# Column tiles, two-head key tails, eight single PSUM banks and a new order in a Performer and mixer kernel

## Chip, cores and metric

The kernel runs on one core of a Trainium2 chip. The metric is the device time of one execution in microseconds (us), as the median of several. The kernel before takes 291.5 us, the median of three runs (291.33 to 291.67).

## What is computed

Eight batches go through linear attention with random features (eight heads, sequence 576, head size 64, 128 features) and then, as a 576 x 512 matrix per batch, through a mixer: a two-layer MLP over tokens (576 to 256 to 576), added to its input, then one over channels (512 to 1536 to 512), added to its input.

```python
def phi(x):
    proj = np.einsum('bhsd,md->bhsm', x, omega)
    h = proj - np.sum(x * x, axis=-1, keepdims=True) / 2.0
    h = h - np.max(h, axis=-1, keepdims=True)
    return np.exp(h) / np.sqrt(m)
q_p, k_p = phi(q * scale), phi(k * scale)
kv = np.einsum('bhsm,bhsd->bhmd', k_p, v)
z = np.sum(k_p, axis=2)
x = np.einsum('bhsm,bhmd->bhsd', q_p, kv) / (np.einsum('bhsm,bhm->bhs', q_p, z)[..., None] + 1e-06)
...
h = np.maximum(x.transpose(0, 2, 1) @ w_tok1, 0.0) @ w_tok2
u = x + h.transpose(0, 2, 1)
out = u + np.maximum(u @ w_ch1, 0.0) @ w_ch2
```

The maximum in phi cancels for q. For k it is divided out row by row: the kernel takes the maximum of the exponentials, and scales v's row and a column of ones by its reciprocal.

## The kernel before

The 576 tokens are 512 main tokens and 64 tail tokens. Every matmul operand is fp16; accumulation is in fp32 in PSUM[...]. The kernel holds six single banks (`bank`, L227) and one `pair` of two (L228).

All work is written as jobs for a planner (L38 to L174): each has an engine, a cost, a key, jobs it depends on, and buffers it takes and gives back. At build time the planner runs a model of the engines: it always picks the job that can start first, and of equals the one with the lowest key. So the order on each engine comes from the costs, the keys (L17 to L20) and the number of buffers, and it is fixed in the program. Until the first heavy channel matmul, the planner fills gaps on TensorE (PE) longer than 0.3 us with dummy matmuls on zeros (L925). A row-tiled job just after another has its key lowered by `ks` (L119).

Per batch and pair of heads (`attention`, L504):

- `kp` (L617) and `qp` (L631) project two heads' k and q on the features. k and q lie transposed, in two halves of 64 partitions, so each matmul uses 64 rows of the array, and two of them run side by side in row tiles.
- ScalarE (ACT) takes the exponential out of PSUM (L500). VectorE (DVE) takes k's maxima (`km`, L643) and reciprocals; GpSimd (POOL) scales v (`vs`, L650).
- `kv` (L663) sums k'v over the main tokens. L670 adds the tails: the tail rows of four heads stand in 128 rows (two tokens of each head in the halves `e`), so each pair of heads needs two matmuls of 130 columns, against `vbd`, v's tails laid out block by block for four heads by POOL (L577).
- `num` (L698, L700) is the numerator with its denominator as a 65th column; DVE divides (L707, L708). From batch 2 on both heads of a pair go into one `pair` of banks and are divided together; in batches 0 and 1 each head has a bank of its own.

k's tails have their own projection `kt` (L532), from `ktt`, a copy that POOL makes out of the transposed k (L366). The tails of q are `qt` (L592). Both write the `pair`.

Batches 0 and 1 are loaded as they are, and PE transposes them (L471, L491). From batch 2 on (`dma_in`), POOL's queue casts q and k to fp16 into DRAM (L355), and SP's queue reads them back transposed (L363). POOL's DMAs are issued in program order and rotate over eight lanes, so one waits until the DMA eight places before it has landed.

The token MLP (`token_mix`, L730; `token_mix_first` for batch 0, in blocks of 128 columns, L781 to L799) gives `u`; SP transposes u by DMA (L762) into `uT`. The 64 tail tokens of two batches are done together in `token_tail` (L807): `w2t` holds the 64 tail columns of w_tok2 twice, once padded to the left half of 128 columns and once to the right, so batch `2p` lands in rows 0 to 63 of one bank and batch `2p + 1` in rows 64 to 127, by four full matmuls. The channel MLP (`channel_mix`, L823) is L832 (first layer, 12 blocks), L852 (relu on ACT), L870 (second layer) and L879 (sum on DVE); SP stores the result. The main tokens of the eight batches take eight passes of it, the tails of all batches a ninth.

POOL's queue also makes two small copies (`touch`, L373, and `touch_u`, L379) that stand between a finished buffer and the next load.

Of the kernel before, what the change touches and what calls it, by code (L numbers as in the profile page):

```python
# [9 lines left out]
FP32 = mybir.dt.float32  # L10
# [6 lines left out]
KEYS = {"a": -1.353, "as": 0.087, "t": -0.936, "ts": 0.381, "gv": 2.14, "lt": -2.027, "lv": -1.831, "to": -1.942, "tt": 0.315, "ks": 1.1, "km": 0.226, "vs": -0.618, "l1": -0.809, "kt": -0.077}  # L17
NEAR = {"1": {"a": -2.195, "as": 0.095, "t": -1.803, "ts": 0.0, "gv": 0.044, "km": -1.819, "vs": -0.475, "kt": -0.001}, "2": {"a": -1.272, "as": 0.154, "t": -0.769, "ts": 0.144, "gv": 1.686, "km": 3.821, "vs": 1.759, "lv": -1.566, "lt": -1.734, "kt": 0.022}}
HEAD = {"kp": [-3.838, -3.822, -3.798, -3.404], "ke": [-2.728, -2.927, -2.827, -2.727], "km": [-4.039, -3.592, -4.221, -2.75], "vs": [-3.332, -3.487, -3.196, -3.14], "qp": [-3.203, -3.403, -3.303, -3.503], "qe": [-3.328, -3.374, -3.028, -3.748], "kv": [-3.533, -3.228, -3.003, -3.133], "ko": [-3.081, -3.035, -3.463, -3.354], "n": [-3.199, -3.199, -3.182, -3.099, -2.999, -3.268, -2.999, -2.899], "no": [-4.124, -3.426, -3.326, -3.144, -3.226, -3.426, -3.126, -2.386], "ktm": -3.64, "kt": -5.022, "kte": -3.991, "qt": -3.751, "qte": -4.323, "kx": [-6.213, -5.658, -5.558, -5.458], "kxo": [-5.931, -7.05, -5.718, -4.783], "ktx": -6.15, "ktxo": -5.753, "qx": [-5.449, -2.792], "qxo": [-4.073, -3.081], "qtx": -5.093, "qtxo": -3.371, "t1": [-0.475, -0.755, -0.539, -0.445], "re": [-0.129, -0.781, 0.181, 0.341], "ut": [-0.17, -0.48, -0.104, -0.64], "uo": [-0.099, -0.259, -0.108, 0.211], "vbd": -8.97, "w1": -9.8, "w1t": -9.38, "w2t": -8.94, "wa": -9.39, "wb": -9.17, "w2": -8.13}
# [18 lines left out]
class Planner:  # L38
# [37 lines left out]
    def run(self):  # L76
# [6 lines left out]
        while any(waiting.values()):  # L83
            choice = None
            for eng, jobs in waiting.items():
                ready = []
                for j in jobs:
# [31 lines left out]
                    key = j.key - (KEYS["ks"] if eng == "PE" and j.rows and last_rows else 0.0)  # L119
# [58 lines left out]
def kernel(  # L178
# [40 lines left out]
    def ring(n, shape, dt, name):  # L219
# [3 lines left out]
             "kvsb": 3, "ktt": 2, "x": 3, "r1": 3, "u": 3, "uT": 3, "r3": 2, "o": 4, "bank": 6, "pair": 1}  # L223
# [4 lines left out]
    pairs = [pspool.tile([P, 2, 512], FP32, name=f"pair{i}") for i in range(COUNT["pair"])]  # L228
# [7 lines left out]
    mask = sb([P, 4], FP16, "mask")  # L236
    w1m = sb([P, NJ, DT], FP16, "w1m")
    w1t = sb([P, 2, DT], FP16, "w1t")
    w2t = sb([P, NT, 2, P], FP16, "w2t")
# [53 lines left out]
    def pair(name):  # L293
        return pairs[place("pair", name)]

# [44 lines left out]
    def load_v_tail(b, key, deps=()):  # L340
        jobs = []
        for g in range(2):
            def tails(g=g):
                nc.gpsimd.dma_start(
                    out=t_vt[place("vt", b)][:, g, :],
                    in_=v[b, 4 * g : 4 * g + 4, SM:S, :].rearrange("h (r e) d -> h r (e d)", e=2),
                )
            jobs.append(dma("POOL", key + 0.01 * g, 0.22, tails, take=[("vt", b)], deps=deps, cost=0.7))
        ld["vt", b] = jobs[-1]

    def load_transposed(b, key, deps=()):
        casts = []
        for n, w in enumerate("qk"):
            def cast(w=w):
                nc.gpsimd.dma_start(  # L355
                    out=scratch[w, b].rearrange("(p r) e -> p (r e)", p=P),
                    in_=src[w][b].rearrange("h s d -> (h s d)").rearrange("(p f) -> p f", p=P),
                )
            casts.append(dma("POOL", key + 0.01 * n, 3.2, cast, deps, cost=0.55))
        for n, w in enumerate("qk"):  # L360
            def back(w=w):
                t = (t_qT if w == "q" else t_kT)[place(w + "T", b)]
                nc.sync.dma_start_transpose(out=t.unsqueeze(1), in_=scratch[w, b])  # L363
            ld[w + "T", b] = dma("SP", key + 0.2 + 0.01 * n, 2.2, back, deps=casts, take=[(w + "T", b)], cost=2.5)
        def ktt():
            nc.gpsimd.tensor_copy(out=t_ktt[place("ktt", b)].rearrange("p (h r) -> p h r", h=H),  # L366
                                  in_=t_kT[place("kT", b)].rearrange("p (h r) -> p h r", h=H)[:, :, R:RA])
        ld["ktt", b] = add("POOL", 0.4, key + 0.25, ktt, deps=[ld["kT", b]], take=[("ktt", b)], give=[("kT", b)])
# [41 lines left out]
    j_mask = add("DVE", 0.7, -8.0, lambda: [nc.vector.memset(mask, 0.0)] + [nc.vector.memset(mask[32 * i : 32 * i + 32, i : i + 1], 1.0) for i in range(4)])  # L410
    j_w1tz = add("DVE", 0.3, -7.9, clear(w1t))
    j_w2tz = add("DVE", 0.3, -7.8, clear(w2t))
# [45 lines left out]
    def rows_of(b, w):  # L458
        return (t_qT if w == "q" else t_kT)[place(w + "T", b)].rearrange("p (h r) -> p h r", h=H)
# [44 lines left out]
    def attention(b, key, step):  # L504
# [15 lines left out]
        def two(n):  # L520
            return [pair(n)[:, e] for e in range(2)]
        def two_of(n):
            return [("pair", n)]
        if dma_in:
            j_ktt = ld["ktt", b]
        else:
            j_ktt = tr["kt", b]
        def kt():
            ps, t = two(n_kt), t_ktt[place("ktt", b)]
            for g in range(2):  # L530
                for e in range(2):
                    nc.tensor.matmul(ps[e][:, g * M : (g + 1) * M], t[half[e], g * P : (g + 1) * P], omT[half[e]], start=True, stop=True)  # L532
        j_kt = add("PE", mm(2, P), k0, kt, deps=[j_ktt, j_omT], take=[*two_of(n_kt), ("kpt", b)], give=[("ktt", b)], rows=True)
        if b == 0:
# [6 lines left out]
            for e in range(2):  # L541
# [4 lines left out]
                j_kte.append(add("ACT", 0.45, kkt, kt_exp, deps=[j_ktm], take=[("kpt", b)], give=[("pair", n_kt)]))  # L546
# [11 lines left out]
        else:  # L558
            def kt_exp():
                exp(t_kpt[place("kpt", b)].rearrange("p g e m -> p e g m"), pair(n_kt)[:, :, 0 : 2 * M].rearrange("p e (g m) -> p e g m", g=2))  # L560
            j_kte = [add("ACT", 0.5, kkt, kt_exp, deps=[j_kt], take=[("kpt", b)], give=[("pair", n_kt)])]
            def kt_max():
# [3 lines left out]
                with nc.allow_low_precision(reason="fp16 operand of the matmul"):  # L566
                    nc.vector.reciprocal(out=rc, in_=mx)
                nc.vector.tensor_tensor(  # L568
                    out=vb[:, :, :, D],
                    in0=rc.unsqueeze(2).broadcast_to((P, 4, 4)),  # L570
                    in1=mask.unsqueeze(1).broadcast_to((P, 4, 4)),
                    op=ALU.mult,
                )
            j_ktm = add("DVE", 1.2, kkt + 0.01, kt_max, deps=[*j_kte, j_mask], take=[("vbd", b)])
            def vbd():
                vb = t_vbd[place("vbd", b)]
                nc.gpsimd.tensor_tensor(  # L577
                    out=vb[:, :, :, 0:D],
                    in0=t_vt[place("vt", b)].rearrange("p g (e d) -> p (g e) d", e=2).unsqueeze(2).broadcast_to((P, 4, 4, D)),
                    in1=vb[:, :, :, D : D + 1].broadcast_to((P, 4, 4, D)),  # L580
                    op=ALU.mult,
                )
            j_vbd = add("POOL", 1.95, kkt + 0.02, vbd, deps=[j_ktm, ld["vt", b]], give=[("vt", b)])
# [10 lines left out]
        def qt_exp():  # L594
            o = t_qpt[place("qpt", b)][:, ST : ST + SM].rearrange("p (h r e) -> p e h r", h=H, e=2)
            exp(o, pair(n_qt)[:, :, 0:256].rearrange("p e (h r) -> p e h r", h=H))
        j_qte = [add("ACT", 0.5, kqe, qt_exp, deps=[j_qt, j_pads], take=[("qpt", b)], give=[("pair", n_qt)])]

        last_x = []
        for hp in range(NU):  # L600
# [57 lines left out]
            def kv(hp=hp, n_kv=n_kv):  # L658
# [10 lines left out]
                for e in range(2):  # L669
# [4 lines left out]
            j_kv = add("PE", mm(8, 65) + mm(2, 130), at_["kv"], kv, deps=[j_v, *j_tail, *je], take=[("bank", n_kv), ("kvsb", (b, hp))],  # L674
# [10 lines left out]
            alone = b < NPE  # L685
            for hs in ((0,), (1,)) if alone else ((0, 1),):
                n_h = (n_n, hs)
                at = ("bank" if alone else "pair", n_h)
                def where(n_h=n_h, hs=hs):
                    return bank(n_h).unsqueeze(1) if len(hs) == 1 else pair(n_h)  # L690
# [116 lines left out]
    def token_tail(pair_, key, jr, jx):  # L807
        n = ("htt", pair_)
        def go():
            ps = bank(n)  # L810
            for o in range(2):
                for tb in range(NT):
                    nc.tensor.matmul(ps, w2t[:, tb, o, :], t_r1[place("r1", 2 * pair_ + o)][:, tb, :],  # L813
                                     start=(o == 0 and tb == 0), stop=(o == 1 and tb == NT - 1))
        j1 = add("PE", mm(4, 512), key, go, deps=[*jr, j_w2t], take=[("bank", n)], give=[("r1", 2 * pair_), ("r1", 2 * pair_ + 1)])
# [82 lines left out]
    def w2t_copy():  # L898
        for o in range(2):
            nc.gpsimd.tensor_copy(out=w2t[:, :, o, o * ST : (o + 1) * ST], in_=w2[:, :, SM:S])  # L900
    j_w2t = add("POOL", 0.6, HEAD["w2t"], w2t_copy, deps=[j_w2, j_w2tz])
# [7 lines left out]
    for b in range(B):  # L909
        if b >= NPE:  # L910
            load_transposed(b, b + key_of("lt", b), [touched.get(b - 2)])
            load_v_tail(b, b + key_of("lt", b) + 0.02)
            load_v(b, b + key_of("lv", b), [ld["ktt", b]] + ([touch_u(1, b + key_of("lv", b) - 0.1, added[1])] if b == NPE else []))
# [44 lines left out]
```

## Time and profile before

| what | us |
|---|---|
| median of three runs | 291.5 |
| the profiled execution | 291.6 |
| its span, first to last instruction | 289.8 |
| channel MLP, first layer, L832, full tokens: matmuls x duration | 376 x 0.379 |
| channel MLP, second layer, L870, 512 columns | 420 x 0.380 |
| tail part of kv, L670, 130 columns | 64 x 0.219 |
| tails of token mixing, L813, 512 columns | 16 x 0.380 |
| ACT exponential of 128 x 512, L500, mean | 0.61 to 0.62 |
| DVE division of a pair of heads, L707 and L708 | 0.215 and 0.824 |
| DVE division of one head, L707 and L708 | 0.187 and 0.492 |
| POOL `vbd`, L577 | 1.928 |
| POOL `ktt`, L366 | 0.398 |
| POOL issue of v's tails, L344 | 0.708 |

The durations of matmuls overlap, since a matmul starts before the one ahead of it has drained; differences of starts tell what one costs. The profile names lines of the kernel before. The granted clock of PE was full throughout.

### The profile page before, as it was taken

To read this page: it belongs to the slowest core of one execution; us is meant where nothing else is said; L and a number is where in the kernel's file an instruction comes from. 1 tells how busy PE (TensorE), PEld (TensorE's weight loads), DVE (VectorE), ACT (ScalarE), POOL (GpSimd) and SP (SyncE) were. 2 spreads that over 40 slices of the span, in tenths; PEclk is the share of its full clock that TensorE was granted. 3 is DMA by queue.
4 is the path that set the end of the run, shared out by engine and by line. 5 is a ranking of instruction groups with operands and counts; after the bars stand their busy time and mean duration, and the time that the engine had idled before them with its cause. 6 is when DMAs were issued, how large, how long until landed. Compare 5 with 4: busy or idle time off the path is not lost.

```text
span 289.8 us, 5517 instructions
## 1 busy us (share of the span) xinstructions
PE 283.2 (98%) x2207; PEld 143.6 (50%) x2207; DVE 147.9 (51%) x280; ACT 153.3 (53%) x307; POOL 91.0 (31%) x116
## 2 busy tenths in 40 slices
PE   8999999999999999999999999999999999999993
PEld 4576454445544544465445544554455444444442
DVE  3985974476469524854657246645565231111012
ACT  2993981298367554855466646653765402512600
POOL 8995920247017401740274016501430000000000
PEclk9999999999999999999999999999999999999999
DMA  8999999799975997999767976998511043012014
GB/s 193 190 199 189 203 226 171 138 220 175 162 125 143 191 118 144 185 193 193 99 153 156 211 100 110 189 199 128 119 74 38 0 96 123 2 49 112 2 35 109
DMA packets 75737, 39.57 MB, mean 137 GB/s; under 512 B 54976, under 2 KB 70720, under 8 KB 75328
## 3 DMA queue, kind: packets, MB, share of 16 engines
q0 software_dynamic: 24304, 17.43, 41.2%
q1 hardware_dynamic: 50624, 21.01, 33.0%
q10 hardware_dynamic: 784, 0.79, 0.9%
q8 instruction: 17, 0.28, 0.4%
q14 instruction: 8, 0.07, 0.1%
HBM read 35.88 MB, written 16.52 MB: 181 GB/s over the span
## 4 chain that ended last, share of the span: by engine, by line
PE 93%; ACT 3%; DMA 1%; issue 0%; DVE 0%; DVEq 0%
PE bank L870 33%; PE bank L832 31%; PE bank L737 4%; PE bank L754 4%; PE bank L617 3%; PE bank L663 3%; PE bank L631 2%; PE pair L698 2%; PE bank L471 2%; ACT kp L500 1%; PE bank L813 1%; PE bank L670 1%; PE bank L738 1%; ACT qp L500 1%; DMA omega_nat<-in_omega_dram 1%; PE bank L781 1%
## 5 line engine op out<-in xcount | busy, mean ns | idle before, releaser
L870 PE MATMUL bank<-wc,r 128*128 128x512 f16 (+2 forms) x444 | 101.5, 374 | 0.0
L852 ACT ACTIVATE r<-bank 128x512 f16<-128x512 f32 x106 | 63.4, 602 | 70.3 <-PE bank L832 69.7
L832 PE MATMUL bank<-uT,wc 128*128 128x512 f16 x376 | 90.1, 379 | 0.3 <-ACT kp L500 0.2
L870 PEld LDWEIGHTS <-r 128*128 128x128 f16 x444 | 40.4, 98 | 47.5 <-issue 5.1
L832 PEld LDWEIGHTS <-wc 128*128 128x128 f16 x424 | 39.3, 98 | 42.4 <-issue 1.2
L500 ACT ACTIVATE qp<-bank 128x512 f16<-128x512 f32 x64 | 35.7, 624 | 13.9 <-PE bank L631 13.8
L643 DVE TENSOR_REDUCE km<-kp 128x8 f16<-128x1024 f16 x32 | 38.6, 1208 | 7.7 <-ACT kp L500 7.7
L500 ACT ACTIVATE kp<-bank 128x512 f16<-128x512 f32 x64 | 34.3, 611 | 10.5 <-PE bank L617 10.5
L650 POOL TENSOR_TENSOR vs<-v,vs 128x512 f16<-128x512 f16 x32 | 33.5, 1057 | 15.4 <-DVE vs L645 11.9
L879 DVE TENSOR_TENSOR o<-u,bank 128x512 f32<-128x512 f16 x28 | 19.1, 681 | 28.1 <-PE bank L870 28.1
L757 DVE TENSOR_TENSOR u<-x,bank 128x512 f16<-128x512 f16 x28 | 17.4, 683 | 9.1 <-PE bank L754 9.1
L577 POOL TENSOR_TENSOR vbd<-vt,vbd 128x1024 f16<-128x1024 f16 x7 | 13.5, 1928 | 26.9 <-DVE vbd L568 23.3
L366 POOL COPY ktt<-kT 128x256 f16<-128x256 f16 x6 | 2.4, 398 | 58.1 <-DMA kT<-k 58.1
L708 DVE TENSOR_TENSOR x<-pair,rc 128x640 f16<-128x640 f32 x24 | 19.8, 824 | 0.8
L707 DVE RECIPROCAL rc<-pair 128x10 f32<-128x10 f32 x24 | 5.2, 215 | 22.4 <-PE pair L700 22.4
L698 PEld LDWEIGHTS <-qp 128*128 128x128 f16 x256 | 12.9, 98 | 6.1 <-issue 0.4
L745 DVE TENSOR_SCALAR r<-bank 128x512 f16<-128x512 f32 x7 | 4.8, 692 | 19.1 <-PE bank L738 19.1
L737 PE MATMUL bank<-x,w1m 128*128 128x512 f16 x56 | 14.4, 379 | 0.0
L663 PEld LDWEIGHTS <-kp 128*128 128x128 f16 x256 | 11.1, 98 | 5.4 <-ACT qp L500 0.6
L663 PE MATMUL bank<-vs,kp 128*128 128x65 f16 x256 | 13.0, 193 | 0.4 <-ACT qp L500 0.4
L754 PE MATMUL bank<-r,w 128*128 128x512 f16 x56 | 13.2, 379 | 0.0
L617 PE MATMUL bank<-omT,kT 64*128 64x128 f16 x256 | 12.1, 218 | 0.0
(109 smaller groups left out, 276.9 us busy)
## 6 DMA issues: line engine op xcount, KB each, us to landing
out_dram<-o SPq DMA_DIRECT2D x32, 256.0 KB, 2.5
q<-in_q_dram POOLq DMA_DIRECT2D x6, 576.0 KB, 6.8
k<-in_k_dram POOLq DMA_DIRECT2D x6, 576.0 KB, 10.0
wc<-in_moe_w_ch_dram POOLq DMA_DIRECT2D x4, 768.0 KB, 10.9
v<-in_v_dram POOLq DMA_DIRECT2D x6, 512.0 KB, 5.9
r<-in_q_dram POOLq DMA_DIRECT2D x4, 256.0 KB, 7.6
v<-in_v_dram POOLq DMA_DIRECT2D x4, 256.0 KB, 7.5
out_dram<-o SPq DMA_DIRECT2D x5, 128.0 KB, 2.4
```

The costliest lines, as they stand in the source:

```text
L500: nc.scalar.activation(out=out, in_=in_, func=AF.Exp, bias=0.0, scale=1.0)
L617: nc.tensor.matmul(ps[e][:, c : c + M], m[half[e], r, :], omT[half[e]], start=True, stop=True)
L643: nc.vector.reduce_max(out=mx, in_=kpv, axis=AX.X)
L650: nc.gpsimd.tensor_tensor(out=vs[:, :, 0:D], in0=t_v[place("v", b)][:, hh[0] : hh[0] + 2, :].rearrange("p h (j d) -> p (h j) d", d=D), in1 ...
L663: nc.tensor.matmul(ps[:, i, :], kpv[:, 2 * i + j // 2, j % 2, :], vs[:, i * NJ + j, 0 : D + 1], start=(i == 0 and j == 0), stop=False, ski ...
L708: nc.vector.tensor_tensor(out=t_x[place("x", b)][:, :, (2 * hp + hs[0]) * D : (2 * hp + hs[0] + n) * D].rearrange("p j (i d) -> p i j d", ...
L737: nc.tensor.matmul(ps, w1m[:, j, tb * P : (tb + 1) * P], x[:, j, :], start=(j == 0), stop=False)
L754: nc.tensor.matmul(ps, w2_of(tb, j), r1[:, tb, :], start=(tb == 0), stop=(tb == NT - 1))
L832: nc.tensor.matmul(ps, wc1[:, db, cb * P : (cb + 1) * P], moving(db), start=(db == 0), stop=(db == ND - 1))
L852: nc.scalar.activation(out=o, in_=bank(n), func=AF.Relu)
L870: nc.tensor.matmul(ps[:, cols], r3[:, cb, j * P : (j + 1) * P], wc2[:, cb, cols], start=(cb == 0), stop=(cb == NCB - 1))
L879: nc.vector.tensor_tensor(out=t_o[place("o", (c, j))][:, cols], in0=uu[:, cols], in1=bank(n)[:, cols], op=ALU.add)
```

## The change

- `token_tail` uses w2's 64 tail columns as they are, for two column tiles: batch `2p` writes PSUM rows 0 to 63 and batch `2p + 1` rows 64 to 127, alternating. The buffer `w2t`, its clearing and its copies go.
- From batch 2 on, k's tails lie by two heads in 128 rows. The cast of k becomes three DMAs: two for the tails (heads 0 to 3, and 4 to 7, side by side in the scratch tensor), and one for the main tokens. `kt` reads the tail part of the transposed k, so POOL's copy `ktt` is not made. The tail part of kv is one matmul for a pair of heads; `vbd` covers two heads for each pair (`mask2`), and v's tails are loaded to match it. Batches 0 and 1 keep the old layout.
- PSUM is eight single banks. Exponentials of k's and q's tails become two instructions each, one for a bank. All numerators go head by head and are divided head by head.
- The keys of the planner are new throughout, and the key bonus `ks` needs the same kind of tiles as the job before. The order on every engine is new. Dummy matmuls become 26 instead of 20.

```diff
-                    key = j.key - (KEYS["ks"] if eng == "PE" and j.rows and last_rows else 0.0)
+                    key = j.key - (KEYS["ks"] if eng == "PE" and j.rows and last_rows == j.rows else 0.0)
...
-             "kvsb": 3, "ktt": 2, "x": 3, "r1": 3, "u": 3, "uT": 3, "r3": 2, "o": 4, "bank": 6, "pair": 1}
+             "kvsb": 3, "ktt": 2, "x": 3, "r1": 3, "u": 3, "uT": 3, "r3": 2, "o": 4, "bank": 8}
...
-                nc.gpsimd.dma_start(
-                    out=t_vt[place("vt", b)][:, g, :],
-                    in_=v[b, 4 * g : 4 * g + 4, SM:S, :].rearrange("h (r e) d -> h r (e d)", e=2),
-                )
+                if b < NPE:
+                    o, i = t_vt[place("vt", b)][:, g, :], v[b, 4 * g : 4 * g + 4, SM:S, :].rearrange("h (r e) d -> h r (e d)", e=2)
+                else:
+                    o = t_vt[place("vt", b)][g * ST : (g + 1) * ST].rearrange("p a (c d) -> p (a c) d", c=2)
+                    i = v[b, :, SM:S, :].rearrange("(a i) t d -> i t a d", i=2)[g]
+                nc.gpsimd.dma_start(out=o, in_=i)
...
-            casts.append(dma("POOL", key + 0.01 * n, 3.2, cast, deps, cost=0.55))
+            def cast_main(w=w):
+                nc.gpsimd.dma_start(
+                    out=scratch[w, b][0 : H * R].rearrange("(p r) e -> p (r e)", p=P),
+                    in_=src[w][b, :, 0:SM, :].rearrange("h s d -> h (s d)").rearrange("h (c f) -> h c f", c=P // H),
+                )
+            def cast_tail(w=w):
+                for g in range(2):
+                    nc.gpsimd.dma_start(
+                        out=scratch[w, b][H * R : H * RA, g * D : (g + 1) * D],
+                        in_=src[w][b, 4 * g : 4 * g + 4, SM:S, :],
+                    )
+            if w == "k":
+                casts.append(dma("POOL", key + 0.01 * n - 0.005, 0.8, cast_tail, deps, cost=1.1))
+            casts.append(dma("POOL", key + 0.01 * n, 3.2, cast if w == "q" else cast_main, deps, cost=0.55))
...
-        def ktt():
-            nc.gpsimd.tensor_copy(out=t_ktt[place("ktt", b)].rearrange("p (h r) -> p h r", h=H),
-                                  in_=t_kT[place("kT", b)].rearrange("p (h r) -> p h r", h=H)[:, :, R:RA])
...
-            ps, t = two(n_kt), t_ktt[place("ktt", b)]
+            ps, t = two(n_kt), t_kT[place("kT", b)][:, H * R : H * RA] if dma_in else t_ktt[place("ktt", b)]
...
-            j_kte = [add("ACT", 0.5, kkt, kt_exp, deps=[j_kt], take=[("kpt", b)], give=[("pair", n_kt)])]
+            nh = 2 if dma_in else 4
+            msk, j_msk = (mask2, j_mask2) if dma_in else (mask, j_mask)
+            j_kte = []
+            for e in range(2):
+                def kt_exp(e=e):
+                    o = t_kpt[place("kpt", b)]
+                    exp(o[:, e] if dma_in else o[:, :, e], two(n_kt)[e][:, 0 : 2 * M].rearrange("p (g m) -> p g m", g=2))
+                j_kte.append(add("ACT", 0.3, kkt, kt_exp, deps=[j_kt], take=[("kpt", b)], give=[("bank", (n_kt, e))]))
...
-                    in0=t_vt[place("vt", b)].rearrange("p g (e d) -> p (g e) d", e=2).unsqueeze(2).broadcast_to((P, 4, 4, D)),
-                    in1=vb[:, :, :, D : D + 1].broadcast_to((P, 4, 4, D)),
+                    in0=t_vt[place("vt", b)].rearrange("p g (e d) -> p (g e) d", e=2).unsqueeze(2).broadcast_to((P, 4, nh, D)),
+                    in1=vb[:, :, :, D : D + 1].broadcast_to((P, 4, nh, D)),
...
-                for e in range(2):
+                if dma_in:
+                    nc.tensor.matmul(ps, kt_[:, hp // 2, hp % 2, :], vb[:, hp, 0:2, 0 : D + 1], start=False, stop=True, skip_group_check=True)
+                for e in () if dma_in else range(2):
                     nc.tensor.matmul(
...
-            alone = b < NPE
-            for hs in ((0,), (1,)) if alone else ((0, 1),):
+            for hs in ((0,), (1,)):
...
-            for o in range(2):
-                for tb in range(NT):
-                    nc.tensor.matmul(ps, w2t[:, tb, o, :], t_r1[place("r1", 2 * pair_ + o)][:, tb, :],
-                                     start=(o == 0 and tb == 0), stop=(o == 1 and tb == NT - 1))
-        j1 = add("PE", mm(4, 512), key, go, deps=[*jr, j_w2t], take=[("bank", n)], give=[("r1", 2 * pair_), ("r1", 2 * pair_ + 1)])
+            for tb in range(NT):
+                for o in range(2):
+                    nc.tensor.matmul(ps[half[o]], w2[:, tb, SM:S], t_r1[place("r1", 2 * pair_ + o)][:, tb, :],
+                                     start=(tb == 0), stop=(tb == NT - 1))
+        j1 = add("PE", mm(2, 512), key, go, deps=[*jr, j_w2], take=[("bank", n)], give=[("r1", 2 * pair_), ("r1", 2 * pair_ + 1)], rows="cols")
```

In the changed file `kt` is L540, `qt` L605, `kp` L632, `qp` L646, `kv` L678 with its tails L685 (batches 2 to 7) and L687, the numerators L714 and L716, the token tails L829, the channel MLP L848 and L886.

## The prediction

> **What bounds the kernel now.** I read the busy shares first, then the chain that ended last, then busy time by stretch, then TensorE in order of time, and last the queues that feed it. The page:
>
> ```profile
> PE 283.2 (98%) x2207; PEld 143.6 (50%) x2207; DVE 147.9 (51%) x280; ACT 153.3 (53%) x307; POOL 91.0 (31%) x116
> ...
> PE 93%; ACT 3%; DMA 1%; issue 0%; DVE 0%; DVEq 0%
> ```
>
> The chain is TensorE. Ends of matmuls are modelled, so I asked for stretches (start:end, length, busy time of PE, PEld, DVE, ACT, POOL, clock, DMA share, GB/s):
>
> ```profile
> 0.00:24.50 24.50, 22.61 (x251) 15.04 (x252) 16.46 (x48) 16.67 (x42) 22.49 (x36) 1.00 1.17 192
> 24.50:62.00 37.50, 37.18 (x337) 19.27 (x335) 23.77 (x50) 21.02 (x43) 12.78 (x17) 1.00 1.12 185
> 62.00:285.00 223.00, 223.00 (x1618) 109.02 (x1617) 107.00 (x183) 115.57 (x224) 55.70 (x65) 1.00 0.66 123
> ```
>
> From 62 us on PE is never idle, and from 24.5 to 62 it lacks 0.3 us. So there time goes only with PE's own work; in the first 24.5 us it goes with what feeds PE. What a step of PE costs is read from starts (start us, us, engine, line):
>
> ```profile
> 60.22 0.38 PE L870 MATMUL bank<-wc,r 128*128 128x512 f16 x1
> 60.53 0.40 PE L617 MATMUL bank<-omT,kT 64*128 64x128 f16 x8
> 60.86 1.04 PE L813 MATMUL bank<-r,w2t 128*128 128x512 f16 x4
> 61.83 0.39 PE L631 MATMUL bank<-qT,omT 64*128 64x512 f16 x2
> 62.20 1.24 PE L832 MATMUL bank<-uT,wc 128*128 128x512 f16 x5
> ```
>
> The second column is modelled; the first is not. Four L813 start at 60.86 and the next thing at 61.83: 0.97 = 4 x 0.216 + 0.10. From L870 to L617 it is 0.31 = 0.216 + 0.095. So a 128x512 matmul takes 0.216 us, and each change between full and row-tiled matmuls about 0.094. The same differences give 57 ns for a 130-column matmul, 29 ns for one of 65 columns.
>
> **The skill.** The Trainium skill, "TensorE: Matmul & The Clock Gate", section "Measured speedup vs the span model", has tiles side by side last as long as one, plus about 4 ns for each further, columns within 5 ns of rows. The trace agrees for rows (both L631 matmuls start 3 ns apart); it shows no column tiles. "TensorEngine Tiling (Array Packing)", "Key Properties", says a change of mode drains the array: the trace's 0.094 us. Its "Restrictions" say column tiling turns fast weight load off: not shown here, a load is 98 ns under a 216 ns matmul. "DMA: Bandwidth & Descriptors", "Why small descriptors are slow (HBM only)", charges every descriptor a fixed part, 27% at 256 bytes; the trace has no load in rows of 256 bytes; v's tails, 32 KB in rows of 512, take 9.6 us to land, mostly in the queue.
>
> **The change part by part.** PE's work, from the changed instruction order times those durations:
>
> 1. k's tails by two heads: 24 of 64 130-column matmuls go (batches 2 to 7): 24 x 0.057 = -1.37.
> 2. Tails of token mixing: four times 4 x 0.216 = 0.86 becomes two pairs of 0.22, 0.44: -1.70 in all. If columns did not overlap: 0; if they go faster than one stream: excluded. First weight load in the open at worst 4 x 0.1. I take -1.70.
> 3. Changes of mode: row visits fall from 43 to 38, four column visits come, three of them touching row visits; borders 86 to 80: -6 x 0.094 = -0.56. A row/column border was never traced; between 0 and 0.19 each; I take 0.094.
>
> Sum -3.63. All numerators, projections and mixing stay.
>
> Times in the new order, below, are PE's instructions in their new order with these durations laid end to end from the point that I work out next; where a feeder is later than that, I add a wait by hand.
>
> The start. In the old order PE begins batch 1's transposes of k (L471) at 24.54 with all four token-mix blocks of batch 0 done; in the new order two blocks (each 4 x 0.109 + 0.216 + 0.22 = 0.87) come later. Equal progress would be 24.54 - 1.74 = 22.80. ACT and DVE feed PE there. ACT's list up to its second scaling of a head is the same, but one relu (0.27) moves behind that scaling and qp's tail is split in two (+0.1): it ended at 20.02, so now near 19.9. On it waits a product of the first token mix (10 matmuls of 56 ns, 0.56); then stand a second product, a block, a third product whose last head DVE has near 21.2, and a block: 19.95 + 3 x 0.56 + 2 x 0.87 = 23.4. k of batch 1 has to be there too: issued at 13.00, 10.0 us to landing, 23.0. On POOL, vbd (1.9) now goes ahead of w1 and w2, and k's issue slips by 0.2; the DMA engines are full meanwhile (share 1.17), which hides it; without that cover it is 0.2 more, still in time. So 23.4 against 22.80: +0.6 (0 to +1.2).
>
> Behind it stand two dummy matmuls, 0.216 each: +0.43. Gone are three waits of the old order by starts: 0.36 at 28.04 and 0.19 at 30.75 for exponentials, 0.06 at 61.8: -0.61; eight single banks let all of batch 1's kp go before the first c1. ACT then has eight exponentials from 25.6 at 0.49, and each bank that PE takes next is free 0.5 to 2 us before.
>
> New waits. (a) Batch 1's k/v sums stand at 39.5 on PE (34.95 before). POOL now issues q, k's two tails and k of batch 2 before its work, and these reuse DMA lanes: the last waits for v's first half of batch 1 (23.25 + 7.5 to 8.5, near 31.8). Then 4 x 1.05 for vs, one 0.7 issue and vbd 1.9 after all of them: 31.8 + 0.3 + 0.55 + 4.2 + 0.7 + 1.9 = 39.45, and the wake-up. +0.1 (0 to +0.6). Queued behind the waiting matmuls is all of PE. (b) SP's first output store now stands ahead of both transposes of batch 2, and it waits for c2:
>
> ```profile
> 45.24 3.26 SPq L363 DMA_TRANSPOSE qT<-q  x1
> 48.55 2.70 SPq L363 DMA_TRANSPOSE kT<-k  x1
> 53.61 1.70 SPq L762 DMA_TRANSPOSE uT<-u  x1
> ...
> 61.91 0.18 POOL L373 COPY junk<-uT 128x1 f16<-128x1 f16 x1 [6.76 <-DMA uT<-u]
> ```
>
> The old order was at its limit here: uT is there at 61.9 and c1 starts at 62.20. The first line becomes about 48.9 (c2's first block at 47.5, copy 0.7, store 0.35), k 52.1, u 54.9; u itself is ready near 54.6, since t2 stands 1.2 later on PE. With the same 8.3 us it lands at 63.2; c1 of batch 1 would start at 62.6. +0.6 (0 to +1.6). qp of batch 2 (56.2) and kp (59.3) still find q (48.9 + 5.8) and k (52.1 + 4.8).
>
> Single numerators: DVE pays 8 x 0.63 (0.49 and 0.19, start to start) instead of 4 x 1.04 (0.82 and 0.22) a batch, 0.9 more, under the 2.7 us between the last numerator and the token mix. Split exponentials: under 2 us in all on a 53% ACT. POOL a batch: ktt copy -0.40, vbd 1.93 to about 1.0, two tail casts +1.4 (nearest row 0.71 each): +0.1. Taking v of a batch earlier than before costs nothing while its buffer is free. These hide under PE; for leaks over six batches I put +0.3 (0 to +1.5).
>
> Sum: -3.63 + 0.6 + 0.43 - 0.61 + 0.1 + 0.6 + 0.3 = -2.2. The profiled execution took 291.6 us (span 289.8, 1.8 around it), so 289.4; the median shown is 0.1 lower: 289.3.
>
> **Rivals.** (1) The waits don't come: without (a), (b) and leaks, 1.0 less: 288.3. For it: PE's order leaves all feeders a us or more except at those two places. Against: at both, the sums above have the feeder later than PE. (2) Columns run one after the other: +1.7, 291.0, no change. For it: never traced here. Against: row tiles overlap. (3) Slower: k's tails, 512 pieces of 256 bytes in two casts ahead of k's main cast, make kT late. Its old arrivals are where POOL copied ktt: 81.16, 112.96, 137.65, 167.70, 197.48, that is 18.8, 19.6, 17.8, 17.1, 16.8 us after q's issue. In the new order PE's kt stands at 84.8, 114.9, 140.3, 170.6, 200.4 (1.2 to 1.3 of start and waits in it), and POOL can issue q, after uT and the vs that stand before it, at about 63.6, 93.4, 118.6, 149.6, 179.4: 21.2, 21.5, 21.7, 21, 21 us for it. The casts should add 1 to 2 us (twice 0.71 of issue, of which q's 6 to 7 us in the queue hide most, and 512 small pieces), so the margins of batches 3 and 4 are then about 0 to 1.4. If they add 4 us, the waits are 1.6, 2.1, 0.1, 0.1, 0 = 3.9, less the leak already counted 0.3: 292.9. It passes the old time from 3.4 us on, since only the first two margins are used up by then. For it: DMA share 0.66 leaves queues, a 32 KB load of v's tails takes 9.6 to land. Against: most of that is waiting behind k, and k's bytes stay the same. (4) DVE becomes late for every token mix: 0.9 more and margins of 1.5 at batch 2: 0.3 a batch at most, 291.1.
>
> **How the numbers follow.** Forecast 0.58 (289.3, own range 288.3 to 290.6), no waits 0.22 (288.3), columns serial or DVE late 0.08 (291.0), k's tails late 0.12 (292.9). A measurement of this kernel can tell 0.2%, 0.6 us. The range 287.7 to 291.2 leaves out the slow rival and a bit at each end. Faster by over 0.2% (under 290.9): 0.57 + 0.22 = 0.79 and nearly 0.01 of the third; same 0.08; slower 0.12.
>
> **What would show it.** PE busy down, its L685 matmuls 24 with 57 ns between starts; L829 starting 4 ns apart in pairs, 0.44 us a visit (0.86 refutes part 2). First transposes of batch 1 near 23.4. PE's idle at kv near 39.5 and before c1 of batch 1 near 62.6; uT's landing. kT's landing against kt at 84.8, 115, 140, 171, 200: a PE wait there is the slow rival. I am wrong if PE shows idle above 3 us after 25.

## The result, and the profile after

The changed kernel takes 306.41 us (median of 4 runs, 302.48 to 309.14), against 291.41 (291.00 to 291.67) for the kernel before, run beside it. A run more than 1.5% above the fastest of its kernel counts as slow, and the ratios, and the medians from here on, leave such runs out. Two of the changed kernel remain (302.48 and 304.78), with a median of 303.63 us and a ratio of 1.042, 95% interval 1.035 to 1.049: 12.2 us more than before, where 289.3 in all was forecast. The profiled execution took 308.05 us with a span of 305.8, so the waits below are longer in sum than those 12.2 us.

The page of the changed kernel, its lines of busy time and of the chain:

```profile
PE 284.5 (93%) x2189; PEld 142.5 (47%) x2189; DVE 152.3 (50%) x330; ACT 154.1 (50%) x322; POOL 92.7 (30%) x120
...
PE 72%; DMA 19%; POOL 4%; DVE 2%; issue 1%; SPq 0%; POOLq 0%; DVEq 0%
```

PE's busy time hardly moved (283.2 before), but the chain is now DMA for a fifth of the span, where it was 1%. Busy time by stretch, the columns as in the prediction:

```profile
24.50:62.00 37.50, 37.50 (x339) 19.20 (x338) 23.00 (x48) 21.55 (x48) 13.68 (x17) 1.00 1.16 189
62.00:100.00 38.00, 32.64 (x244) 15.37 (x243) 21.76 (x45) 19.51 (x42) 13.47 (x16) 0.91 1.03 130
100.00:140.00 40.00, 38.12 (x336) 19.58 (x333) 22.99 (x53) 23.27 (x51) 17.37 (x23) 1.00 1.12 154
140.00:180.00 40.00, 35.84 (x262) 17.11 (x258) 19.89 (x42) 20.18 (x41) 10.31 (x13) 0.96 0.92 131
180.00:220.00 40.00, 36.94 (x281) 18.18 (x281) 20.32 (x41) 20.80 (x43) 10.32 (x13) 1.00 1.03 153
```

Up to 62 us PE is as busy as forecast, and from 220 on it is busy without a break. Between, PE lacks 14.5 us, and the clock (the third column from the end) is below 1 in two stretches. What it lacks is named by the list of what PE waited for (us in all, times, longest); L540 projects k's tails, L646 projects q:

```profile
PE bank L540 <- DMA kT<-k: 7.2, 3, 4.2
PE bank L646 <- DMA qT<-q: 5.6, 2, 3.8
```

Five waits, one in each of batches 3 to 7, for the transposes of q or k. By starts they are 3.83, 1.95, 4.23, 1.65 and 1.55 us, 13.2 in all ("by starts" is the distance from one matmul's start to the next, less what the first costs: 0.216 us for 512 columns, and 0.095 for a change of mode). Transposes are late, then, and the queues say from where on. DMA issues of the kernel before, with size and median us from issue to landing:

```profile
v<-in_v_dram POOLq DMA_DIRECT2D x6, 512.0 KB, 5.9
...
qT<-q SPq DMA_TRANSPOSE x6, 7.1
kT<-k SPq DMA_TRANSPOSE x6, 4.8
```

and the same lines of the changed kernel:

```profile
v<-in_v_dram POOLq DMA_DIRECT2D x6, 512.0 KB, 14.1
...
qT<-q SPq DMA_TRANSPOSE x6, 13.7
kT<-k SPq DMA_TRANSPOSE x6, 7.9
```

The loads of v and the transposes got slower together: 2.4 times as long for v, 1.9 for qT, 1.6 for kT. POOL in order of time shows why they meet. Batch 4 before, where v is L335:

```profile
112.96 0.40 POOL L366 COPY ktt<-kT 128x256 f16<-128x256 f16 x1 [15.69 <-DMA kT<-k]
113.30 0.93 POOL L335 DMA_DIRECT2D v<-in_v_dram  x1
```

and after, where v is L331:

```profile
103.24 1.72 POOL L364 DMA_DIRECT2D k<-in_k_dram  x2
104.94 0.56 POOL L358 DMA_DIRECT2D k<-in_k_dram  x1
105.49 1.27 POOL L345 DMA_DIRECT2D vt<-in_v_dram  x2
106.75 0.93 POOL L331 DMA_DIRECT2D v<-in_v_dram  x1
```

Before, POOL stood 15.7 us at `ktt` until kT had landed, and the load of v, next in its queue, stood there too. The change takes `ktt` away, and nothing on POOL waits for kT any more: v goes out right behind the casts of k, 0.7 us before SP issues the transpose of qT (107.47). In the planner the load still depends on kT's job, but that sets an order in a plan only; it makes no semaphore. The key of this load, `lv`, which the change lowers by almost two batches, plays no part: with its old values the changed kernel's order of instructions is the same on every engine.

The Trainium skill, "DMA: Bandwidth & Descriptors", section "Issuing engines are not separate DMA queues", says that DMAs of the scalar, sync and gpsimd engines run on the same 16 DMA engines and interleave. The figures above agree: a load issued by POOL and transposes issued by SP, with no dependency between them, take longer together. (Not all of v's longer time is due to the transposes: in batch 4 k's cast and v's tails, ahead of it in POOL's queue, land at 114.5 to 116.0 us only, v at 121.0, and qT at 121.8.)

### The profile page after: what moved, and what is told of

It is laid out like the page before. It is cut to its first block, busy times and chain, and to the rows that moved or that the text cites. A ratio compares the mean times of both kernels' runs of the same rounds, so it can differ in the third digit from the quotient of the medians.

```text
span 305.8 us, 5601 instructions
## 1 busy us (share of the span) xinstructions
PE 284.5 (93%) x2189; PEld 142.5 (47%) x2189; DVE 152.3 (50%) x330; ACT 154.1 (50%) x322; POOL 92.7 (30%) x120
## 4 chain that ended last, share of the span: by engine, by line
PE 72%; DMA 19%; POOL 4%; DVE 2%; issue 1%; SPq 0%; POOLq 0%; DVEq 0%
PE bank L886 29%; PE bank L848 22%; DMA qT<-q 9%; DMA kT<-k 8%; PE bank L678 2%; PE bank L646 2%; PE bank L714 2%; PE bank L632 2%; PE bank L753 2%; PE bank L770 2%; DMA vt<-in_v_dram 2%; POOL vs L665 1%; DVE km L658 1%; PE bank L829 1%; POOL vbd L559 1%
## 5 line engine op out<-in xcount | busy, mean ns | idle before, releaser
L886 PE MATMUL bank<-wc,r 128*128 128x512 f16 (+2 forms) x444 | 103.5, 379 | 0.0
L848 PE MATMUL bank<-uT,wc 128*128 128x512 f16 x376 | 88.5, 379 | 0.2 <-DMA uT<-u 0.2
L886 PEld LDWEIGHTS <-r 128*128 128x128 f16 x444 | 41.0, 98 | 49.9 <-issue 7.7
L848 PEld LDWEIGHTS <-wc 128*128 128x128 f16 x424 | 39.6, 98 | 44.1 <-issue 0.8
L508 ACT ACTIVATE kp<-bank 128x512 f16<-128x512 f32 x64 | 34.8, 645 | 10.7 <-PE bank L632 10.7
L590 POOL TENSOR_TENSOR vbd<-vt,vbd 128x512 f16<-128x512 f16 (+1 forms) x7 | 8.2, 1176 | 95.5 <-DVE vbd L581 95.5
L724 DVE TENSOR_TENSOR x<-bank,rc 128x320 f16<-128x320 f32 x62 | 30.5, 492 | 2.1
L723 DVE RECIPROCAL rc<-bank 128x5 f32<-128x5 f32 x62 | 11.3, 183 | 15.8 <-PE bank L716 15.8
L646 PE MATMUL bank<-qT,omT 64*128 64x512 f16 x64 | 12.2, 394 | 5.6 <-DMA qT<-q 5.6
L761 DVE TENSOR_SCALAR r<-bank 128x512 f16<-128x512 f32 x7 | 4.8, 692 | 23.4 <-PE bank L754 23.4
L714 PEld LDWEIGHTS <-qp 128*128 128x128 f16 x256 | 12.6, 98 | 5.7
L678 PE MATMUL bank<-vs,kp 128*128 128x65 f16 x256 | 12.9, 193 | 1.8 <-POOL vs L665 1.7
L678 PEld LDWEIGHTS <-kp 128*128 128x128 f16 x256 | 11.4, 98 | 6.7 <-issue 2.1
L753 PE MATMUL bank<-x,w1m 128*128 128x512 f16 x56 | 14.4, 380 | 0.0
L770 PE MATMUL bank<-r,w 128*128 128x512 f16 x56 | 14.3, 398 | 0.0
L714 PE MATMUL bank<-kvsb,qp 128*128 128x65 f16 x256 | 13.6, 194 | 0.0
```

The costliest lines, as they stand in the source:

```text
L508: nc.scalar.activation(out=out, in_=in_, func=AF.Exp, bias=0.0, scale=1.0)
L678: nc.tensor.matmul(ps[:, i, :], kpv[:, 2 * i + j // 2, j % 2, :], vs[:, i * NJ + j, 0 : D + 1], start=(i == 0 and j == 0), stop=False, ski ...
L714: nc.tensor.matmul(ps[:, k, j * 65 : (j + 1) * 65], st, s[:, i, 0 : D + 1], start=True, stop=True)
L724: nc.vector.tensor_tensor(out=t_x[place("x", b)][:, :, (2 * hp + hs[0]) * D : (2 * hp + hs[0] + n) * D].rearrange("p j (i d) -> p i j d", ...
L753: nc.tensor.matmul(ps, w1m[:, j, tb * P : (tb + 1) * P], x[:, j, :], start=(j == 0), stop=False)
L770: nc.tensor.matmul(ps, w2_of(tb, j), r1[:, tb, :], start=(tb == 0), stop=(tb == NT - 1))
```

## Experiments

Theory A: the lost wait sends v's load beside the transposes, and makes them late. Theory B: the small pieces of k's tails do. Theory C: the new order makes PE wait. The first four runs set these against each other, two from either kernel.

**x1_gate_kT.** The changed kernel with the wait given back:

```diff
         def main():
+            if b >= NPE:
+                nc.gpsimd.tensor_copy(out=junk[:, b : b + 1], in_=t_kT[place("kT", b)][:, H * RA - 1 : H * RA])
             nc.gpsimd.dma_start(out=t_v[place("v", b)][:, h0:h1, :], ...
```

> The changed kernel with one instruction more in each of batches 2 to 7: ahead of the load of v, POOL copies one column of kT of the same batch, so the load is issued only when kT's transpose has landed, as in the kernel before. The order on every engine is otherwise that of the changed kernel. Theory A (the load of v, which lost its wait, runs beside the transposes of qT and kT and makes them late): 288 to 290 us, transposes back to about 7 us, PE busy in nearly all of 62 to 220. Theory B (the 512 pieces of 256 B in k's tails and v's tails delay the casts and transposes): 304 to 307 us, transposes still late. Theory C (the new order of instructions is what makes PE wait): 304 to 307 us too, with transposes on time and PE waiting elsewhere.

Measured: 290.64 us (22 runs), ratio to the kernel before 0.998 (0.9967 to 0.9993), 0.6 us above theory A's bracket. One instruction of 0.19 us a batch takes back all that the change had lost, and a little more. Its POOL, again batch 4:

```profile
117.92 0.19 POOL L332 COPY junk<-kT 128x1 f16<-128x1 f16 x1 [13.90 <-DMA kT<-k]
118.04 0.91 POOL L333 DMA_DIRECT2D v<-in_v_dram  x1
```

and its landings:

```profile
v<-in_v_dram POOLq DMA_DIRECT2D x6, 512.0 KB, 7.2
...
qT<-q SPq DMA_TRANSPOSE x6, 8.7
kT<-k SPq DMA_TRANSPOSE x6, 4.5
```

All three are near the kernel before, and PE has no wait over 0.25 us by starts from 31 us on. This execution (294.3 us) lost 5 us ahead of that: 1.4 and 2.7 of waits, for the exponentials of batch 0 and the load of batch 1's k, and the rest at half the clock behind the second. Theories B and C fall as sole causes: the pieces are still there, and the order is the same but for the copy.

**x4_gate_qT.** The copied column is of qT instead of kT.

> As the first kernel, but the one column that POOL copies is of qT: the load of v is issued when qT has landed, and runs beside the transpose of kT only. Theory A: qT back to about 7 us after its issue, kT still late (some 7 to 10 us); 289 to 297 us, above the kernel gated on kT. Theory B or C: 304 to 307 us.

Measured: 292.81 us, ratio 1.0047 (1.0031 to 1.0063). The time is as expected for A, but not for its reason: qT landed in a median of 8.4 us and kT in 4.6, not late. SP issues kT's transpose right behind qT's (in batch 3 it is done with that at 82.07), and v goes out only at 82.82, when qT has landed. Its PE waits are others: 1.4 us for POOL's products of v and 1.2 us for a copy of batch 1's q.

**x2_before_ungated.** The kernel before, with v's load ahead of `ktt`, not behind it:

```diff
         def ktt():
+            v_load(b, 0, H)
             nc.gpsimd.tensor_copy(out=t_ktt[place("ktt", b)]...
```

> The kernel before with the load of v issued ahead of the copy of k's tails, not behind it, in batches 2 to 7: two instructions of POOL swapped, nothing else moved. Theory A: 300 to 306 us, with gaps of PE of 1.5 to 4 us at q's or k's first use of batches 3 to 7. Theories B and C: 291 to 292 us, since neither the pieces nor the order of the changed kernel are in it.

Measured: 293.80 us, ratio 1.0084 (1.0064 to 1.0105). A miss: the transposes were late here too (10.7 and 6.9 us), but only 2.5 us came of it; PE waited 0.45 and 1.7 us by starts, for `ktt` in batches 4 and 5.

**x3_before_pieces.** The kernel before, with the small casts doubled into memory that nothing reads:

```diff
             def cast(w=w):
+                for g in range(2 if w == "k" else 0):
+                    nc.gpsimd.dma_start(out=extra[b][:, g * D : (g + 1) * D], in_=src[w][b, 4 * g : 4 * g + 4, SM:S, :])
                 nc.gpsimd.dma_start(
```

> The kernel before with k's tails cast a second time in the changed kernel's form (two casts of 256 pieces of 256 B ahead of each cast of k, batches 2 to 7) into memory that nothing reads. Theory A: 291.4 to 293 us: each pair takes 1 to 2 us of the software queue, and k's transposes come some 2 us later without PE waiting long. Theory B: 298 to 305 us.

Measured: 292.22 us, ratio 1.0053 (1.0031 to 1.0074); qT 8.7 us, kT 4.9. As A had it: the pieces alone cost 0.9 us, not 13.

So in the changed kernel the wait is worth 13.0 us, and in the kernel before the same freedom costs 2.5. Either v was still held back there by what stands ahead of it on POOL, or the loss needs a partner. Three runs on that.

**x5_before_v_early.** As x2_before_ungated, but v goes out behind the cast of k, from batch 3 on:

```diff
+                if w == "k" and b > NPE:
+                    v_load(b, 0, H)
```

> The kernel before with the load of v of batches 3 to 7 issued directly behind the cast of k, some 10 us or more ahead of where x2_before_ungated has it. Theory A1 (a load of v beside the transposes makes them late in either kernel, and x2_before_ungated lost only 2.5 us because POOL's products of v still held its load back): 298 to 306 us, with PE gaps of 1.5 to 4 us in most of batches 3 to 7. Theory A2 (the loss takes the load of v and something else of the change together, the pieces or the earlier use of q and k): 292 to 296 us.

**x8_before_v_early_pieces.** That edit and the one of x3_before_pieces.

> x5_before_v_early with the doubled casts of k's tails of x3_before_pieces. Theory A1: 299 to 308 us, some 1 us above x5_before_v_early, the price of the pieces alone. Theory A2 with the pieces as the other half: 302 to 308 us, while x5_before_v_early stays under 296. Theory A2 with the earlier use of q and k as the other half: 293 to 297 us.

**x6_after_whole_k.** The changed kernel, v not gated, with the cast of k whole (`cast` in place of `cast_tail` and `cast_main`).

> The changed kernel, its load of v without a wait, with k cast in one piece as before, so that the 512 small pieces are gone; k's tails then lie in the old places and the kernel multiplies other rows of k than it should, at the same times. Theory A1: 302 to 306 us, about the changed kernel less 1 us. Theory A2 with the pieces: 290 to 295 us. Theory A2 with the earlier use of q and k: 300 to 306 us.

Measured: 292.78 us for x5_before_v_early, ratio 1.0047 (1.0029 to 1.0066); 300.91 for x8_before_v_early_pieces, 1.0309 (1.0271 to 1.0346), just under A2's bracket; 297.25 for x6_after_whole_k, 1.0166 (1.0145 to 1.0187), between the two brackets of A2. It is theory A2, with the pieces as a partner, though x6_after_whole_k keeps more of the loss than the pieces' bracket gave it. With a run told further below, both orders can be set side by side:

| us | v behind kT | v early |
|---|---|---|
| order before, k whole | 291.3 | 292.8 |
| order before, with pieces | 292.2 | 300.9 |
| changed order, k whole | 289.4 (x10_gate_whole_k) | 297.3 |
| changed order, with pieces | 290.6 | 303.6 |

In the order before, the two cost 0.9 and 1.5 alone and 9.6 together; in the changed order 1.2 and 7.9 alone and 14.2 together. So 7 us in the one and 5 in the other belong to neither alone. Both are rough: x2_before_ungated has 2.5 for early v, and the last two cells of the right column rest on five runs over 4 us and on two over 2.

The waits of PE for qT show how that comes about (us in all, times, longest). x5_before_v_early:

```profile
PE bank L636 <- DMA qT<-q: 1.1, 2, 0.8
```

x8_before_v_early_pieces:

```profile
PE bank L639 <- DMA qT<-q: 5.6, 2, 3.0
```

x3_before_pieces has no such line. Slack is here the time from a transpose's landing to PE's first use of it. For q in batches 3 and 4 it is about 4.1 us each in the kernel before and 1.3 each with the pieces: they make q some 2.8 us later, and PE does not wait. Early v uses up the slack and goes 0.4 and 0.9 us beyond it, by starts, so it makes q 4.5 and 4.9 us later. With both, q is 6.8 and 7.2 us later, nearly the sum; what is over the slack, 2.66 and 3.11 us, is what PE waits.

In the changed order v alone goes past the slack. x6_after_whole_k:

```profile
PE bank L536 <- DMA kT<-k: 4.9, 1, 4.9
PE bank L642 <- DMA qT<-q: 4.6, 2, 3.8
```

There is less of it (x10_gate_whole_k: 3.8 and 2.5 us for q in batches 3 and 4, 3.4 for k in batch 5, where the kernel before has 4.8), but above all the delay is greater: 7.7 and 3.4 us for q, 8.3 for k, where x5_before_v_early has 4.5, 4.9 and 3.5. The issues of v and qT of batch 3, x5_before_v_early first:

```profile
61.72 0.95 POOL L334 DMA_DIRECT2D v<-in_v_dram  x1
68.61 7.51 SPq L368 DMA_TRANSPOSE qT<-q  x1
```

```profile
71.62 0.93 POOL L331 DMA_DIRECT2D v<-in_v_dram  x1
71.69 3.72 SPq L370 DMA_TRANSPOSE qT<-q  x1
```

Where v has a head start it lands first (76.9 us, qT 81.7); where they go out together they land together (86.5 both; in batch 5, with v 2.1 us behind, 148.2 both). The changed order sends v out close to qT. One thing more of the change stays in x6_after_whole_k and x10_gate_whole_k and was not tried alone: v's tails, which now come in 512 rows of 64 values a batch, as many and as small as the pieces of k.

The rest is the clock. A stretch of x8_before_v_early_pieces around its second wait, at a mean clock of 0.89:

```profile
115.00:130.00 15.00, 11.96 (x75) 4.94 (x73) 6.56 (x13) 7.13 (x14) 3.69 (x5) 0.89 0.94 131
```

and one of the changed kernel, right behind its wait of batch 3:

```profile
88.00:92.00 4.00, 4.00 (x16) 1.24 (x14) 0.77 (x2) 1.74 (x4) 0.00 (x0) 0.50 0.42 119
```

Here PE is busy without a break and at half its clock: 512-column matmuls start 427 ns apart, not 216. Set start against start with x10_gate_whole_k, which has the same order, the changed kernel lost 2.5 us that way behind its wait of 3.83 and 1.6 behind that of 4.23; x8_before_v_early_pieces, against x3_before_pieces, lost 1.6 behind each of its two. The changed kernel's 13.2 of waits, 4.1 of clock and 1.9 at c1 of batch 1 (c1 is the first layer of the channel MLP) and at batch 2's products of v make 19.2; it was 0.3 ahead before them, so its last matmul starts 18.8 us behind that of x10_gate_whole_k. That one is 2.9 ahead of the kernel before (below): 15.9 of the 16.0 by which the span grew.

**x10_gate_whole_k.** The gated kernel with k's cast whole.

> The changed kernel gated on kT, with k cast in one piece as before; k's tails then lie in the old places and the kernel multiplies other rows of k than it should, at the same times. It prices the small pieces alone under the gate. If they are the smaller partner that only matters beside the load of v: within 1 us of the gated kernel, 289.6 to 290.8 us. If they delay on their own: 287.5 to 289 us.

Measured: 289.41 us, ratio 0.994 (0.9919 to 0.996), 1.2 us under the gated kernel (x1_gate_kT); neither bracket holds, and it lies nearer to the first. Its trace shows no PE wait over 0.3 us after 4 us.

**x11_before_columns.** The kernel before with the change's loop of `token_tail` and nothing else.

> The kernel before with the tails of token mixing in two column tiles and nothing else of the change. Four pairs of batches each spend two passes of 0.216 us less on PE, 1.7 us in all, and pay two borders of some 0.09 us each, 0.7 us in all: 290.3 us if the pairs run at once and PE is the bound; 291.3 us or more if the two tiles run one after the other.

Measured: 290.68 us, ratio 0.9977 (0.9969 to 0.9986). The pairs run at once. The 16 matmuls and the border behind each visit take 2.22 us by starts where they took 3.56, and 0.7 us of the time went, 0.3 less than expected.

**x7_gate_old_head, x9_gate_no_touch_u.** Two tries at the spread of the gated kernel (289.3 to 292.5): the head's keys of the kernel before, and batch 2's load of v without the copy of u ahead of it.

> The changed kernel gated on kT, with the table of keys of the head (batches 0 and 1) taken from the kernel before. If the spread of the gated kernel (289.3 to 292.5 us) comes from its head, where PE stands at batch 1's first transposes until the load of k lands: 288.5 to 290 us with a spread of under 1 us. If not: 290 to 291.5 us, as wide as before.

> The changed kernel gated on kT, without the one-column copy of u of batch 1 that stands ahead of batch 2's load of v, so that this load is issued behind kT of batch 2 alone, up to 3 us sooner. Theory D (what is left of the gated kernel's loss is POOL's products of v of batch 2 coming late, which x4_gate_qT shows as two waits of 0.7 and 0.55 us near 70 us and x7_gate_old_head as one of 1.6 us): 289.3 to 290.2 us, under the gated kernel, and no wait of the numerators of k and v near 70 us. If the rest is the head's: 290.4 to 291 us, unchanged.

Measured: 291.53 us (289.34 to 293.56), ratio 0.9999 (0.9972 to 1.0027), and 290.80 (289.51 to 292.24), ratio 0.9981 (0.9964 to 0.9997). Neither narrows the spread, and the second lies in its bracket for "unchanged". In x9_gate_no_touch_u the waits near 70 us are gone, but a wait of 1.1 us for batch 1's qT, at 37 us, is there, as in x4_gate_qT and not in x1_gate_kT or x10_gate_whole_k. The cause of the spread is open.

**x12_gate_whole_k_right.** The last is a version with k whole and the products right: `ktt` comes back, and two 64-column products bring each pair of heads into 128 rows.

```diff
+                for hp in range(NU):
+                    for e in range(2):
+                        nc.tensor.matmul(ps[hp // 2][half[e], (hp % 2) * M : (hp % 2 + 1) * M], t[half[e], 2 * hp * RT : (2 * hp + 2) * RT],
+                                         omT[half[e]], start=True, stop=True)
```

> A version meant to beat both kernels: the changed kernel with k cast in one piece, k's tails copied out by POOL behind kT's transpose as in the kernel before (this copy is also the wait that the load of v stands behind), and each pair of heads brought into 128 rows by two products of 64 columns on opposite quarters of PE, so that one product of 130 columns a pair of heads still does. Eight products of k's tails a batch in place of four. If the pieces cost what x10_gate_whole_k and the gated kernel differ by (1.2 us) and the products of opposite quarters run at once: 289.3 to 289.9 us. If these products run one after the other, 6 batches x 4 x 0.057 = 1.4 us more: 290.5 to 291 us.

Measured: 291.56 us, ratio 1.0006 (0.9992 to 1.0021). The products of opposite quarters start 3 ns apart, so they do run at once, but there are four pairs a batch in place of two: by starts k's tails take 2.48 us, not 1.15 (x10_gate_whole_k). The expectation had counted that at nothing, and neither of its brackets holds. Its profile has waits in the head only, up to 40 us: by starts 1.3 us for batch 1's k, 1.0 for its q, and 1.1 for POOL's products of batch 0's v. Of all versions with the reference's arithmetic, x1_gate_kT, x9_gate_no_touch_u and x11_before_columns beat both kernels, each by 0.2%.

## Why the prediction was wrong

The step that failed is one sentence on the work hidden under PE: "Taking v of a batch earlier than before costs nothing while its buffer is free." A buffer is not all that a load needs. It needs the DMA engines, and the prediction itself had their share at 1.12 and 1.17 early on and 0.66 on average over the rest. It counted POOL's queue "a batch" as a sum of durations (ktt -0.40, vbd, casts: +0.1), and so took `ktt` for 0.40 us of work, where it was a wait of 10 to 16 us with a 512 KB load behind it. Of the wait that went, it did not ask what had been queued behind it. In its place the runs showed 13.0 us for that wait (303.63 against 290.64), some 5 of which the pieces had to be there for.

The term for the pieces was mis-sized too, on the small side. "Leaks over six batches" were put at +0.3; the pieces cost 0.9 us in the order before and 1.2 in the changed one, where no trace shows the place. Rival 3 was the right kind, transposes late for PE, on the side "slower", but with one cause of two, and its case of 4 us came to 292.9. It priced the pieces at 1 to 2 us of delay, and k's slack shrank by 1.0 and 1.4 in batches 3 and 4 of x3_before_pieces; but it left q out, which came 2.8 us later, and it was q that PE stopped for in these batches. For k it had margins of about 0 to 1.4 there; x1_gate_kT shows 4.1 and 1.7, and 1.1 in batch 5. So little was left that the delay from v came through almost whole.

What held:

- Part 1: 24 of the 130-column matmuls went; the kind took 2.46 us by starts in x10_gate_whole_k, 3.93 before: -1.47 (forecast -1.37).
- Part 2 and its borders: pairs start 3 to 4 ns apart. The four visits take 2.22 us with the border behind each, 3.56 before, -1.34; less four more borders ahead of them, near -1.0 against about -0.95 worked out. As in the skill's section that the prediction cites, columns overlap like rows. The weight loads of the column tiles take 106 to 109 ns in x10_gate_whole_k, where 98 was the rule, and hide under 0.24 us from pair to pair.
- The sum: from first to last matmul, x10_gate_whole_k is 2.93 us shorter than the kernel before. The forecast had -2.2 with 0.3 for leaks and 0.7 for the two waits (a) and (b), which this trace does not have.
- The head of the changed kernel: batch 1's transposes at 23.0 (forecast 23.4); k/v of batch 1 at 39.0 with no wait (39.5); uT 8.6 us after its issue, c1 of batch 1 ready at 62.35 and 0.29 late (forecast 62.6 and 0.6). The first transpose there went out at 48.4; the prediction wrote 48.9, but its own terms, 47.5 + 0.7 + 0.35, make 48.55.
- The mark that was to refute it, "idle above 3 us after 25", is what came.

One more thing was not in the sum. Outside the span a run of the kernel before spends 1.8 us; with the changed head it is 2.2 to 2.5 in every kernel that has it, and 1.9 in x7_gate_old_head. The 0.5 us are part of why 2.9 us less in PE's row became 2.0 of time. They lie outside the records, so no trace shows what they are.

## What to carry to other kernels

An instruction that waits is also a gate for everything behind it in its queue, and above all for transfers, which nothing else may hold back. Before one is taken out, list what is queued behind it and what that will run beside; a planner's dependency that makes no semaphore doesn't take its place. And set delays against the slack, not against the time: two that cost 0.9 and 1.5 us alone cost 9.6 together here, because one of them had already used the slack up.

## What the runs showed of the hardware

A load of 512 KB (as counted in the destination's type) landed in 5.9 to 7.2 us where it went out behind the transposes and in 10.3 to 14.4 beside them; the transposes of q took 6.4 to 9.9 us and 10.7 to 13.7 (medians of a kernel). In the changed kernel and x6_after_whole_k, where v and qT went out less than 2.2 us apart, they landed within 1.2 us of each other.

PE's clock went to half behind waits of 2.66, 3.11, 3.83, 4.23 and 4.99 us by starts, and behind one of 2.7 in the head of x1_gate_kT, but not behind one of 3.88 in x6_after_whole_k, nor after any of up to 1.95. Length alone doesn't decide. The changed kernel behind its wait of batch 3, and x6_after_whole_k behind that of 3.88 (the clock is the third column from the end):

```profile
86.10:92.92 6.82, 5.39 (x25) 1.87 (x25) 1.38 (x2) 2.42 (x7) 0.00 (x0) 0.50 0.52 108
```

```profile
87.00:92.00 5.00, 5.00 (x48) 2.41 (x48) 3.35 (x6) 3.82 (x10) 0.93 (x1) 1.00 0.57 141
```

In these traces the clock changes on a grid of 3.41 us: in the changed kernel at 86.10, 92.92, 154.36 and 157.78, which is 2, 18 and 1 steps apart. It went to half at the end of a step in which PE stood still for 2.0 us or more: 2.4 and 3.2 in the changed kernel, 2.6 and 2.0 in x8_before_v_early_pieces, 2.6 in x1_gate_kT, a whole step in x6_after_whole_k. The grid cut the wait of 3.88 into 2.0 and 1.9, and the clock stayed. The two cases of 2.0 went different ways, so the border lies near there, by these few cases. It came back at the end of a step in which PE stood for 0.1 us at most; after steps with 0.85 and 1.5 it stayed at half. Where the grid lies differs from one execution to the next (first full clock at 4.2 to 7.5 us), so it is in part luck whether a wait of 2 to 4 us costs clock too. The kernel before is also at half until 6.9 us, where its first matmuls start 427 ns apart; "full throughout" holds from there on.

The Trainium skill, "TensorE: Matmul & The Clock Gate", section "What's actually happening", has the rate halve after an idle window of about 3.4 us and come back after as long a busy one. The traces agree on the length and on the way back; for the way down, 2.0 to 2.6 us of standing still within one step was enough here.
